# A quarter of k's transfers on GpSimd's queue, the last stores on SyncE's, and another order of the same work in an attention + feed-forward kernel

## The chip, the cores and the metric

The kernel runs on one core of a Trainium2 chip. The metric is the device time of one execution in microseconds (us), taken as the median of several runs. Lower is better.

## The reference

Attention runs inside chunks of 64 tokens, without a mask, for 8 batches of 8 heads, 576 tokens of 64 numbers each. Its output becomes a matrix x of 4608 tokens by 512, and x goes through a feed-forward layer with a sigmoid form of gelu. All arrays are float32.

```python
q_c = q.reshape(B, H, nc, chunk, D)          # B, H, S, D = 8, 8, 576, 64; chunk = 64, nc = 9
...
scores = scale * np.matmul(q_c, k_c.transpose(0, 1, 2, 4, 3))
scores = scores - np.max(scores, axis=-1, keepdims=True)
attn = np.exp(scores)
attn = attn / (np.sum(attn, axis=-1, keepdims=True) + 1e-09)
out = np.matmul(attn, v_c)
...
x = np.ascontiguousarray(attn_out.transpose(0, 2, 1, 3)).reshape(B * S, H * D)     # 4608 x 512
h = x @ w_in                                                                       # 512 x 2048
g = h * (1.0 / (1.0 + np.exp(-1.702 * h)))
return (g @ w_out).astype(np.float32)                                              # 2048 x 512
```

## The kernel before

**Tiling.** The 4608 tokens are 36 tiles of 128, and nine blocks of four tiles. A float32 product is made from three matmuls on a high and a low part of each operand (lines 1129 to 1131, 1166 to 1168 and 696 to 698). The inner dimension of 2048 is cut into 16 slices. Block n and slice j have the number g = 16 n + j. For each g there is a first product h_g (x times w_in, in the halves `h0_g` and `h_g` of six matmuls), its gelu and split (`gh_g` on ScalarE, `gl_g` on VectorE), and four second products `o_g_t` (three matmuls each, t is the tile of 128 tokens), which add up in the accumulators `po_t` over the 16 slices. At the end of a block `ob_n_t` copies an accumulator to SBUF (ScalarE for even t, VectorE for odd t) and `st_n_t` stores it. Blocks 0 to 2 work in this way. Blocks 3 to 8 are taken two at a time: seven products `P1` to `P7` replace the eight of two blocks and two slices, with weight sums that were prepared (`psum`, `phi`, `plo`), written to the DRAM tensor `seven` (`pout`, `pouts`), and read back piece by piece (`ld`). The drains of these products are called `d0` to `d6`.

**Attention.** Tiles 0 to 3 are done one by one at the start. From tile 4 on they go in pairs, u = 4, 6, ..., 34, so the fourth pair is u = 10. For a pair from u = 6 on, q and k come from DRAM in pieces of 32 by 32 numbers (`qk_0_n_u` is quarter n of q, `qk_1_n_u` quarter n of k; a quarter is four transfers, and eight for u = 16 and 26), VectorE transposes each of the two (`tq0_u` for q, `tq1_u` for k, line 893), TensorE makes the scores (`s_u`, together with the product with v of the pair before), VectorE and ScalarE the softmax (`mx`, `m`, `ex`, `z`), GpSimd divides by the sums (`n_u`, line 939), and VectorE transposes the result (`et0` to `et`, line 958). There is one buffer `raw` for q and k, one for v and one for the transposed pair. So a pair's loads can start only after `tq1` of the pair before. The two PSUM buffers `hp` hold h_g: `h0_g` can start only when `gl_(g-2)` has read its buffer.

**Order.** All steps go into a planner (`Plan`). It keeps a clock per engine with costs written in the code and takes from the ready steps the one with the lowest rank. `ORDER` writes out the first part of each engine's order, and `NUDGE` changes single ranks. What comes out is one fixed order per engine, and each engine works through its own order one by one. "DMA" in the planner is SyncE's queue (SP). SP issues every load and the traffic with `seven`; its transfers share eight semaphores in turn, and a transfer waits until the eighth before it has landed. GpSimd issues the output's stores.

```python
st["raw"] = const.tile([P, 2, NP, 8, 32], F32, tag=raw_tag, name=f"raw_{u}")
...
nc.gpsimd.dma_start(out[b * S + s : b * S + s + c, :], ob[o : o + c])
```

Of the kernel before, what the change touches and what calls it, by code (L numbers as in the profile page):

```python
# [9 lines left out]
F32 = mybir.dt.float32  # L10
# [16 lines left out]
    ),  # L27
    ACT: (
# [13 lines left out]
        "k_1 q_1 k_0 q_0 q_2 k_2 q_3 k_3 raw_0 v_1 v_0 v_2 raw_1 v_3 raw_3 raw_2 rows0_4 "  # L42
        "raw_4 raw_5 raw_7 raw_8 v0_4 v1_4 raw_6"
# [4 lines left out]
class Plan:  # L48
# [9 lines left out]
    ISSUE, LANES, LANDING = 0.48, 8, 1.8  # L58
    PIECES = 3072
    TABLE_LOAD = 1.3  # L60

    def __init__(self, buffers):
        self.free = dict(buffers)
        self.steps = []
        self.landed = [0.0] * self.LANES
        self.flight = []
        self.first = {}
        self.nudge = {}


    def add(self, engine, cost, rank, fn, need=(), make=None, take=(), give=(), table=None, port=False, after=0.0):
        rank += self.nudge.get(make, 0.0)
        self.steps.append((engine, cost, rank, fn, tuple(need), make, tuple(take), tuple(give), table, port or (engine == POOL and not after), after))
# [18 lines left out]
    def emit(self):  # L92
        waits, users, ready = {}, {}, {e: [] for e in self.HANDOVER}
        at = []
# [16 lines left out]
        while left:  # L111
            for e, heap in ready.items():
                while heap and busy[e] <= now + 1e-9:
# [13 lines left out]
                    _, cost, _, fn, _, make, take, give, tab, port, after = self.steps[pick]  # L127
# [18 lines left out]
                    if e != DMA:  # L146
                        post(done, 1, (make, e, True))
                    post(done + self.HANDOVER[e], 1, (make, e, False))
# [24 lines left out]
def tile_chunk_attention_ffn(  # L173
# [38 lines left out]
    RLATE = 0  # L212

    NUDGE = {
# [4 lines left out]
    }  # L219
    ON_POOL = ()  # L220
# [590 lines left out]
    def plan_pair(u):  # L811
        st = {}
        ev = lambda n: f"{n}_{u}"
        pe = u < NPE
        NG = 2 * NP * 2
# [10 lines left out]
        def load_qk(i, n):  # L826

            if i == n == 0:
                st["raw"] = const.tile([P, 2, NP, 8, 32], F32, tag=raw_tag, name=f"raw_{u}")
            t, src = st["raw"], (q, k)[i]  # L830
            at = list(spans(u * P, 2 * P))
            if len(at) == 4:
                b, s = at[0][:2]
                for h in range(2):
                    for d in range(2):
                        p0 = h * 64 + d * 32
                        for half in range(2):
                            c = s + 32 * half
                            nc.sync.dma_start(
# [6 lines left out]
            for b, s, o, c in at:  # L846
                for h in range(2):
                    for d in range(2):
                        p0 = h * 64 + d * 32
                        nc.sync.dma_start(  # L850
# [158 lines left out]
        rank = RANKS[(u - TB) // 2]  # L1009
        if pe:  # L1010
# [290 lines left out]
```

## Time and profile before

| What | Value |
|---|---|
| median of 3 runs (lowest, highest) | 835.79 us (835.48, 837.0) |
| the profiled execution's own time | 833.93 us |
| span of its trace, from the first to the last instruction | 832.2 us |
| TensorE busy in the span | 815.4 us (98%) |
| VectorE, ScalarE, GpSimd busy | 524.4, 370.4, 103.8 us |
| mean granted TensorE clock | 0.998 |

The 1.7 us between the span and the execution's own time lie around the program. TensorE counts as busy from a matmul's start to its modelled end, and one matmul's end overlaps the next one's start; so the distance from start to start shows the pace better than the busy time does. SPq and POOLq are the issuing queues of SyncE and GpSimd. A line with "idle before <-X" says how long the engine had stood idle and what released it. The trace names a tile and not a step, so the steps named in the text follow from the order of the program: "g_l<-hp,g_h" is a `gl`, "qkT<-raw" a `tq`.

### The profile page before, as it was taken

Reading aid. Unit: us, or ns where it says so; the run is one execution under the profiler, and the core shown is the slowest. Engines: PE = TensorE matmul, PEld = TensorE weight load, DVE = VectorE, ACT = ScalarE, POOL = GpSimd, SP = SyncE. Lnnn points to the kernel's source line nnn. Section 1 sums busy time; section 2 is a strip of 40 time slices with the busy share of each in tenths; the row PEclk is TensorE's granted clock in tenths of the full one; section 3 lists DMA queues with packets and bytes.
Section 4 is the critical chain, followed back from the end, with each engine's and each line's share of the span. In section 5 each row is a group of like instructions: output and inputs, shape, how many; then the busy total and the mean of one; then the engine's idle time right before and its main releaser. Section 6 shows DMA issues by size and latency. Waiting matters only on the chain.

```text
span 832.2 us, 14752 instructions
## 1 busy us (share of the span) xinstructions
PE 815.4 (98%) x5750; PEld 674.1 (81%) x5750; DVE 524.4 (63%) x725; ACT 370.4 (45%) x545; POOL 103.8 (12%) x114
## 2 busy tenths in 40 slices
PE   8999998999999999999999999999999999999997
PEld 7888887888887888888888887888888888888786
DVE  5878975564467869874858677867568343434322
ACT  5989824433435537423436244443354223232321
POOL 1000071000166411000001010000011010000101
PEclk9999999999999999999999999999999999999999
DMA  9997855432385456755665237664440054443101
GB/s 255 327 314 209 256 143 116 73 63 34 75 257 130 147 138 202 159 163 152 157 155 154 39 87 203 159 157 128 123 141 13 14 168 131 130 118 99 50 1 50
DMA packets 231332, 114.23 MB, mean 137 GB/s; under 512 B 185952, under 2 KB 208480, under 8 KB 231264
## 3 DMA queue, kind: packets, MB, share of 16 engines
q1 hardware_dynamic: 228320, 103.86, 47.6%
q0 software_dynamic: 2944, 9.44, 3.0%
q8 instruction: 45, 0.74, 0.4%
q14 instruction: 23, 0.19, 0.1%
HBM read 89.13 MB, written 24.12 MB: 136 GB/s over the span
## 4 chain that ended last, share of the span: by engine, by line
PE 60%; issue 20%; SPq 11%; DMA 4%; DVE 2%; ACT 2%; POOL 1%; POOLq 0%; DVEq 0%; ACTq 0%
PE po L1166 10%; PE po L1167 10%; PE po L1168 10%; PE hp L696 6%; PE hp L697 6%; PE hp L698 6%; SPq L850 4%; PE hp L1129 3%; PE hp L1131 3%; PE hp L1130 3%; SPq L274 2%; SPq L354 2%; SPq L278 2%; PE s L909 2%; PE x L983 1%
## 5 line engine op out<-in xcount | busy, mean ns | idle before, releaser
L1166 PE MATMUL po<-w,g_l 128*128 128x512 f32 x576 | 226.9, 394 | 1.4 <-DVE g_l L743 0.8
L1168 PE MATMUL po<-w,g_h 128*128 128x512 f32 x576 | 224.4, 390 | 0.0
L1167 PE MATMUL po<-w,g_h 128*128 128x512 f32 x576 | 224.3, 389 | 0.0
L1166 PEld LDWEIGHTS po<-w,g_l 128*128 128x128 f32 x576 | 108.2, 188 | 26.2 <-DVE g_l L743 2.6
L1168 PEld LDWEIGHTS po<-w,g_h 128*128 128x128 f32 x576 | 108.1, 188 | 22.9
L1167 PEld LDWEIGHTS po<-w,g_h 128*128 128x128 f32 x576 | 108.3, 188 | 21.7
L734 ACT ACTIVATE g<-g 128x512 f32<-128x512 f32 x48 | 30.2, 632 | 137.8 <-DVE g L681 137.6
L696 PE MATMUL hp<-w,w 128*128 128x512 f32 x224 | 87.2, 389 | 0.3 <-DVE f L681 0.3
L698 PE MATMUL hp<-w,w 128*128 128x512 f32 x224 | 87.1, 389 | 0.0
L697 PE MATMUL hp<-w,w 128*128 128x512 f32 x224 | 87.1, 389 | 0.0
L958 DVE STREAM_TRANSPOSE eT<-e 32x512 f32<-32x512 f32 x120 | 84.2, 701 | 3.0 <-POOL e L939 1.2
L1129 PE MATMUL hp<-x_l,w 128*128 128x512 f32 x184 | 72.6, 394 | 4.4 <-DVE g_l L1156 4.4
L1131 PE MATMUL hp<-x_h,w 128*128 128x512 f32 x184 | 72.3, 393 | 0.0
L1130 PE MATMUL hp<-x_h,w 128*128 128x512 f32 x184 | 72.1, 392 | 0.0
L1185 POOL DMA_DIRECT2D out_dram<-ob x39 | 21.7, 557 | 400.3 <-ACT ob L1178 361.6
L939 POOL TENSOR_TENSOR e<-e,r 128x1024 f32<-128x1024 f32 x16 | 31.2, 1952 | 287.5 <-DVE r L936 170.5
L743 DVE TENSOR_TENSOR g_l<-g,g_h 128x512 fp32r<-128x512 f32 x48 | 33.4, 697 | 52.8 <-ACT g_h L739 52.7
L739 ACT ACTIVATE g_h<-g 128x512 fp32r<-128x512 f32 x48 | 30.3, 632 | 76.2 <-PE po L1168 69.6
L893 DVE STREAM_TRANSPOSE qkT<-raw 128x1024 f32<-128x1024 f32 x30 | 37.2, 1241 | 33.7 <-DMA raw<-in_k_dram 18.0
L1156 DVE TENSOR_TENSOR g_l<-hp,g_h 128x512 fp32r<-128x512 f32 (+1 forms) x50 | 33.2, 666 | 38.1 <-ACT g_h L1151 37.8
L1150 ACT ACTIVATE hp<-hp 128x512 f32<-128x512 f32 (+1 forms) x50 | 28.4, 569 | 47.9 <-PE hp L1131 37.8
L696 PEld LDWEIGHTS hp<-w,w 128*128 128x128 f32 x224 | 42.0, 188 | 9.4 <-DVE f L681 0.7
(118 smaller groups left out, 1224.6 us busy)
## 6 DMA issues: line engine op xcount, KB each, us to landing
w<-seven SPq DMA_DIRECT2D x112, 256.0 KB, 2.9
pieces<-seven SPq DMA_DIRECT2D x56, 256.0 KB, 2.9
seven<-w SPq DMA_DIRECT2D x24, 512.0 KB, 3.7
raw<-in_moe_w_in_dram SPq DMA_DIRECT2D x16, 512.0 KB, 7.3
raw<-in_moe_w_out_dram SPq DMA_DIRECT2D x16, 512.0 KB, 7.3
out_dram<-ob POOLq DMA_DIRECT2D x31, 256.0 KB, 2.6
raw<-in_q_dram SPq DMA_DIRECT2D x208, 32.0 KB, 2.2
raw<-in_k_dram SPq DMA_DIRECT2D x208, 32.0 KB, 2.1
```

The source lines that it names most:

```text
L696: nc.tensor.matmul(hp, w[:, 0, c], xl[:, c], start=c == 0, stop=False)
L697: nc.tensor.matmul(hp, w[:, 0, c], xh[:, c], start=False, stop=False)
L698: nc.tensor.matmul(hp, w[:, 1, c], xh[:, c], start=False, stop=c == 1)
L743: nc.vector.tensor_tensor(gl, words(h, late), gh.bitcast(F32), op=ALU.subtract)
L893: nc.vector.transpose(st["tr"][:, i].rearrange("p n (t j) -> p (n t) j", j=32), st["raw"][:, i].rearrange("p n t j -> p (n t) j"),)
L958: nc.vector.transpose(st["et"][po : po + 32, :, 32 * a : 32 * a + 32], st["e"][pi : pi + 32, :, 32 * b : 32 * b + 32],)
L1129: nc.tensor.matmul(hp, wh, xl, start=cc == 0, stop=False)
L1130: nc.tensor.matmul(hp, wh, xh, start=False, stop=False)
L1131: nc.tensor.matmul(hp, wl, xh, start=False, stop=cc == NCC - 1)
L1166: nc.tensor.matmul(po, gl[:, c], w[:, 0, :], start=first, stop=False)
L1167: nc.tensor.matmul(po, gh[:, c], w[:, 0, :], start=False, stop=False)
L1168: nc.tensor.matmul(po, gh[:, c], w[:, 1, :], start=False, stop=last)
```

## The change

From pair u = 10 on the last quarter of k (n = 3) is issued on GpSimd's queue, in single transfers `qkp_..._u` that the planner places on GpSimd: 4 for most pairs, 8 for u = 16 and 26, 60 in all. The four stores of the last block go to SP. The planner has other costs for issue and landing, and a model of GpSimd's queue. A shift for whole pairs (`SHIFT`) and 35 more entries in `NUDGE` give another order of the same steps on all engines. No computing step is added or removed.

```diff
-    ISSUE, LANES, LANDING = 0.48, 8, 1.8
+    ISSUE, LANES, LANDING = 0.495, 8, 1.9
     PIECES = 3072
+    RING = 3
...
+                    if late:
+                        cost += max(0.0, self.ring[-self.RING] - now)
+                        late += min(3.1, max(0.0, 0.5 * (self.landed[-1] - now - cost - 2.0)))
+                        self.ring.append(now + cost + late)
...
+    POOLED, POOL_FROM = 1, 10
...
+        "wj_13": 14, "qk_0_3_10": -6, "o_127_1": -4, "pa0_4": 5, "o_86_1": -12, "P7_0_0": 8,
...
+    SHIFT = {10: 3.5, 8: 2.0, 26: -12.5, 12: 4.0, 34: -12.5, 6: 3.0}
...
+        pooled = POOLED * (u >= POOL_FROM)
...
+        def load_qk(i, n, hd, only=None):
+            queue = nc.gpsimd if i and n >= NP - pooled else nc.sync
...
-                            nc.sync.dma_start(
+                            queue.dma_start(
...
+                    for x in range(4 * count):
+                        parts[i].append(ev(f"qkp_{8 * n + x}"))
+                        plan.add(
+                            POOL, 0.59, rank - ahead - RLATE,
+                            lambda i=i, n=n, x=x: load_qk(i, n, HD[x // count : x // count + 1], x % count if count > 1 else None),
+                            need=[ev("rawt")], make=parts[i][-1], late=1.95,
+                        )
...
-        def o_store(t):
+        def o_store(t, queue):
...
-                nc.gpsimd.dma_start(out[b * S + s : b * S + s + c, :], ob[o : o + c])
+                queue.dma_start(out[b * S + s : b * S + s + c, :], ob[o : o + c])
...
+                if n == NB - 1:
+                    plan.add(DMA, (count, 0.85, 128), rank - STORE, lambda t=t: o_store(t, nc.sync), **store)
+                else:
+                    plan.add(POOL, 0.56 * count, rank - STORE, lambda t=t: o_store(t, nc.gpsimd), after=2.6, late=2.6, **store)
```

Three places of the order follow, each before and then with the change. **VectorE at pair u = 10**, in block 1: `qkT` is the transposed pair, and the two `g_l` ahead of `z` are `gl_16` and `gl_17`.

```order
L926 TENSOR_TENSOR e_1436<-s_1361,m_1437 128x1024
L893 STREAM_TRANSPOSE qkT_1496<-raw_1335 128x1024
L1156 TENSOR_TENSOR g_l_1499<-hp_1466,g_h_1498 128x512
L1156 TENSOR_TENSOR g_l_1525<-hp_1489,g_h_1524 128x512
L933 TENSOR_REDUCE z_1550<-e_1436 128x16
```

With the change, at the same place:

```order
L942 TENSOR_TENSOR e_1440<-s_1364,m_1441 128x1024
L1187 TENSOR_TENSOR g_l_1503<-hp_1472,g_h_1502 128x512
L909 STREAM_TRANSPOSE qkT_1525<-raw_1349 128x1024
L1187 TENSOR_TENSOR g_l_1528<-hp_1495,g_h_1527 128x512
L949 TENSOR_REDUCE z_1551<-e_1440 128x16
```

The first `g_l` (`gl_16`) now stands ahead of q's transpose `tq0_10`; the second (`gl_17`) still stands behind it.

**SP's queue at pair u = 18**, at the end of block 1's loads: `raw` is this pair's q and k, `pieces`, `w` and `seven` are the traffic of the weight sums.

```order
L850 DMA raw_2394<-in_k_dram 32x8x32 x8
L687 DMA pieces<-seven 128x2x256 x2
L689 DMA w_328<-seven 128x512 x2
L689 DMA w_440<-seven 128x512 x2
L617 DMA seven<-w_530 128x1024
L617 DMA seven<-w_543 128x1024
L850 DMA raw_2394<-in_k_dram 32x8x32 x4
L354 DMA v_2680<-in_v_dram 64x8x64 x2
```

With the change, at the same place:

```order
L866 DMA raw_2382<-in_k_dram 32x8x32 x4
L701 DMA pieces<-seven 128x2x256 x2
L703 DMA w_328<-seven 128x512 x2
L703 DMA w_440<-seven 128x512 x2
L631 DMA seven<-w_530 128x1024
L631 DMA seven<-w_543 128x1024
L368 DMA v_2680<-in_v_dram 64x8x64 x2
```

The last four transfers of k, which stood behind six reads from `seven` and two writes to it, are gone from SP. On GpSimd they stand ahead of block 1's first store and of `n_14`. In VectorE's order `tq1_18` has moved from behind `m_16` to ahead of `mx_16`.

**TensorE where blocks 7 and 8 meet**: `po_3` is `o_127_3`, the last second product of block 7 for tile 3. The rows behind it belong to block 8, whose slices 14 and 15 (`o_142`, `o_143`) come first.

```order
L1166 MATMUL po_3_6783<-w_1216,g_l_7471 128x512
L1167 MATMUL po_3_6783<-w_1216,g_h_7470 128x512
L1168 MATMUL po_3_6783<-w_1216,g_h_7470 128x512
L1166 MATMUL po_1_7503<-w_1132,g_l_7481 128x512
L1167 MATMUL po_1_7503<-w_1132,g_h_7480 128x512
L1168 MATMUL po_1_7503<-w_1132,g_h_7480 128x512
L1166 MATMUL po_0_7495<-w_1216,g_l_7508 128x512
```

With the change, at the same place:

```order
L1197 MATMUL po_3_6783<-w_1181,g_l_7465 128x512
L1198 MATMUL po_3_6783<-w_1181,g_h_7464 128x512
L1199 MATMUL po_3_6783<-w_1181,g_h_7464 128x512
L1197 MATMUL po_2_7499<-w_1145,g_l_7492 128x512
L1198 MATMUL po_2_7499<-w_1145,g_h_7491 128x512
L1199 MATMUL po_2_7499<-w_1145,g_h_7491 128x512
L1197 MATMUL po_1_7506<-w_1145,g_l_7492 128x512
L1198 MATMUL po_1_7506<-w_1145,g_h_7491 128x512
L1199 MATMUL po_1_7506<-w_1145,g_h_7491 128x512
L1197 MATMUL po_1_7506<-w_1181,g_l_7504 128x512
```

Between `o_127_3` and the first product with `gl_143` there was one product of `o_142` and are now two. A little ahead of this, behind `P4` of the last slice, five second products stand in front of the first one with `gl_127`, where four stood.

## Rows read from the trace of the kernel before

**Rows 1.** The waits of TensorE: us in total, times, longest.

```profile
PE hp L1129 <- DVE g_l L1156: 4.4, 2, 2.6
...
PE po L1166 <- DVE g_l L743: 0.8, 1, 0.8
...
PE hp L696 <- DVE f L681: 0.3, 1, 0.3
```

**Rows 2.** TensorE's timeline around the first gap: start, length, line, tile.

```profile
125.00 0.39 PE L1131 MATMUL hp<-x_h,w 128*128 128x512 f32 x1
...
128.40 0.39 PE L1131 MATMUL hp<-x_h,w 128*128 128x512 f32 x1
131.36 0.50 PE L1129 MATMUL hp<-x_l,w 128*128 128x512 f32 x1 [2.57 <-DVE g_l L1156]
...
136.03 0.40 PE L1167 MATMUL po<-w,g_h 128*128 128x512 f32 x1
```

**Rows 3.** Busy time by stretch behind that gap; PEclk is the granted clock.

```profile
132.00:136.00 4.00, 4.00 (x12) 3.13 (x11) 1.65 (x3) 1.84 (x3) 1.69 (x1) 0.58 0.39 64
```

**Rows 4.** VectorE's timeline in the first gap.

```profile
129.48 1.25 DVE L893 STREAM_TRANSPOSE qkT<-raw 128x1024 f32<-128x1024 f32 x1 [4.28 <-DMA raw<-in_k_dram]
130.65 1.25 DVE L1156 TENSOR_TENSOR g_l<-hp,g_h 128x512 fp32r<-128x512 f32 x2
```

**Rows 5.** SP's and GpSimd's timelines ahead of it.

```profile
116.20 10.27 SPq L850 DMA_DIRECT2D raw<-in_q_dram  x16
126.51 7.99 SPq L850 DMA_DIRECT2D raw<-in_k_dram  x16
...
116.14 2.54 POOL L581 TENSOR_TENSOR whole<-w 128x512 f32<-128x512 f32 x2
```

**Rows 6.** Line 850 from 116 to 135 us: its transfers' time to landing.

```profile
DMA to landing us min/median/max: 1.8/2.1/4.4
```

**Rows 7.** TensorE's timeline at the second gap.

```profile
250.69 0.39 PE L1168 MATMUL po<-w,g_h 128*128 128x512 f32 x1
252.87 0.50 PE L1129 MATMUL hp<-x_l,w 128*128 128x512 f32 x1 [1.79 <-DVE g_l L1156]
```

**Rows 8.** VectorE's timeline at the second gap.

```profile
249.79 1.25 DVE L893 STREAM_TRANSPOSE qkT<-raw 128x1024 f32<-128x1024 f32 x1 [4.36 <-DMA raw<-in_k_dram]
```

**Rows 9.** SP's timeline ahead of it, and line 850's landing from 240 to 252 us.

```profile
241.44 4.02 SPq L850 DMA_DIRECT2D raw<-in_k_dram  x4
...
DMA to landing us min/median/max: 1.7/4.7/7.6
```

**Rows 10.** TensorE's timeline where blocks 7 and 8 meet.

```profile
778.46 0.39 PE L1168 MATMUL po<-w,g_h 128*128 128x512 f32 x1
778.96 0.50 PE L1166 MATMUL po<-w,g_l 128*128 128x512 f32 x1
...
782.97 0.39 PE L1168 MATMUL po<-w,g_h 128*128 128x512 f32 x1
...
784.13 0.50 PE L1166 MATMUL po<-w,g_l 128*128 128x512 f32 x1 [0.77 <-DVE g_l L743]
```

**Rows 11.** The end: VectorE's last copy and GpSimd's last store.

```profile
827.03 0.69 DVE L1180 COPY ob<-po 128x512 f32<-128x512 f32 x1 [0.67 <-PE po L1168]
828.13 0.55 POOL L1185 DMA_DIRECT2D out_dram<-ob  x1 [0.16 <-issue]
```

**Rows 12.** The page's DMA issues: count, KB each, median us to landing.

```profile
out_dram<-ob POOLq DMA_DIRECT2D x31, 256.0 KB, 2.6
...
seven<-w SPq DMA_DIRECT2D x8, 256.0 KB, 3.6
```

**Rows 13.** Line 1185, all stores from GpSimd: ns min/median/max of an issue.

```profile
L1185 POOL DMA_DIRECT2D out_dram<-ob x39: 534/542/728, 122.3 to 828.1; - x39
```

**Rows 14.** VectorE's and GpSimd's timelines at pair u = 16: `tq1_16` and `n_14`.

```profile
217.86 1.25 DVE L893 STREAM_TRANSPOSE qkT<-raw 128x1024 f32<-128x1024 f32 x1 [1.87 <-DMA raw<-in_k_dram]
...
227.15 1.90 POOL L939 TENSOR_TENSOR e<-e,r 128x1024 f32<-128x1024 f32 x1 [0.54 <-DVE r L936]
```

More of the change, by code (lines that the diff above doesn't have):

```diff
@@ L66, in __init__, with add @@
         self.flight = []
+        self.ring = [0.0] * self.RING
         self.first = {}
         self.nudge = {}
-    def add(self, engine, cost, rank, fn, need=(), make=None, take=(), give=(), table=None, port=False, after=0.0):
-        rank += self.nudge.get(make, 0.0)
-        self.steps.append((engine, cost, rank, fn, tuple(need), make, tuple(take), tuple(give), table, port or (engine == POOL and not after), after))
+        self.shift = 0.0
+    def add(self, engine, cost, rank, fn, need=(), make=None, take=(), give=(), table=None, port=False, after=0.0, late=0.0):
+        rank += self.nudge.get(make, 0.0) + self.shift
+        self.steps.append((engine, cost, rank, fn, tuple(need), make, tuple(take), tuple(give), table, port or (engine == POOL and not late), after, late))
     def bulk(self, cost, rank, fn, need=(), make=None, take=(), give=()):
@@ L126, in emit @@
                         break
-                    _, cost, _, fn, _, make, take, give, tab, port, after = self.steps[pick]
+                    _, cost, _, fn, _, make, take, give, tab, port, after, late = self.steps[pick]
                     if first.get(e):
@@ L146, in emit @@
                     if e != DMA:
-                        post(done, 1, (make, e, True))
-                    post(done + self.HANDOVER[e], 1, (make, e, False))
+                        post(done + late, 1, (make, e, True))
+                    post(done + late + self.HANDOVER[e], 1, (make, e, False))
                     if e == DMA:
@@ L824, in load_qk_rows, with raw_tile @@
             load_rows(st["raw"][:, t], u + t, (q, k))
[L826 to L829 removed]
+        def raw_tile():
+            st["raw"] = const.tile([P, 2, NP, 8, 32], F32, tag=raw_tag, name=f"raw_{u}")
+        def load_qk(i, n, hd, only=None):
+            queue = nc.gpsimd if i and n >= NP - pooled else nc.sync
             t, src = st["raw"], (q, k)[i]
@@ L833, in load_qk @@
                 b, s = at[0][:2]
-                for h in range(2):
-                    for d in range(2):
+                for h, d in hd:
+                    if True:
                         p0 = h * 64 + d * 32
-                        for half in range(2):
+                        for half in range(2) if only is None else (only,):
                             c = s + 32 * half
-                            nc.sync.dma_start(
+                            queue.dma_start(
                                 t[p0 : p0 + 32, i, n, half::2, :],
@@ L845, in load_qk @@
                 return
-            for b, s, o, c in at:
-                for h in range(2):
-                    for d in range(2):
+            for b, s, o, c in at if only is None else at[only : only + 1]:
+                for h, d in hd:
+                    if True:
                         p0 = h * 64 + d * 32
-                        nc.sync.dma_start(
+                        queue.dma_start(
                             t[p0 : p0 + 32, i, n, o // 32 : (o + c) // 32, :],
@@ L1229, in plan_ffn @@
                 )
-                plan.add(
-                    POOL, 0.7 * len(list(spans((n * TB + t) * P, P))), rank - STORE, lambda t=t: o_store(t), need=[f"ob_{n}_{t}"],
-                    make=f"st_{n}_{t}", give=[tag], after=3.2,
-                )
+                count = len(list(spans((n * TB + t) * P, P)))
+                store = dict(need=[f"ob_{n}_{t}"], make=f"st_{n}_{t}", give=[tag])
+                if n == NB - 1:
+                    plan.add(DMA, (count, 0.85, 128), rank - STORE, lambda t=t: o_store(t, nc.sync), **store)
+                else:
+                    plan.add(POOL, 0.56 * count, rank - STORE, lambda t=t: o_store(t, nc.gpsimd), after=2.6, late=2.6, **store)
     def keep_warm(pool, tag, count):
```

32 lines of the change are left out of this document (21 added, 11 removed), and 24 rows, old and new, of tables (NUDGE, ORDER).

## The prediction

> **What bounds the kernel now.** I read the page first: TensorE is busy for 98% of the span, so time can come only from places where it stands or runs slowly, and I looked for those in its list of waits, then in its timeline from start to start. Between waits it is packed: fifteen intervals between 125.00 and 128.40 us give 3.40 / 15 = 0.227 us for each 128x512 matmul [rows 2]. That pace is the floor of all computing, and the change removes no matmul. Behind 40 us the timeline leaves it at four places only; some 6 us more are lost in the start, whose order the change hardly touches, and I put those at nothing either way.
>
> **Place A, block 1, pair u = 10.** TensorE starts a matmul at 128.40 and the next, the first of `h0_18`, at 131.36; it waited 2.57 us for a `gl` [rows 2]. From 128.40 to 136.03 it does 14 intervals, which take 14 x 0.227 = 3.17 us at the pace: 7.63 - 3.17 = 4.46 us are lost. The pause itself is 2.96 - 0.23 = 2.73 of that. The rest is the clock: after the pause the granted clock is 0.58 of full in 132 to 136 us, the lower of two levels (1.2 instead of 2.4 GHz) for most of it [rows 3]. VectorE shows what is late: the transpose `tq0_10` starts at 129.48 after 4.28 us of idle, released by a transfer, and `gl_16` and `gl_17` start behind it at 130.65 (1.25 us for the two) [rows 4]. The row names k's tile line, but both transposes have that line; it is the first one, so it waits for q. SP issued q's sixteen transfers from 116.20 for 10.27 us, then k's for 7.99 us [rows 5], and a transfer lands a median of 2.1 us behind its issue [rows 6]. So a `gl` whose own inputs were there stood in VectorE's queue behind a transpose that waited for a DMA.
>
> **Place B, block 2, pair u = 18.** The pause from 250.69 to 252.87 is 2.18 us, 2.18 - 0.23 = 1.95 lost [rows 7]. Here `tq1_18` starts at 249.79 after 4.36 us of idle, waiting for k [rows 8], and `gl_36` is behind it. SP issued k's last four transfers from 241.44 for 4.02 us, and in this stretch the median landing is 4.7 us and the longest 7.6 [rows 9], against 2.1 at A: they stand behind reads and writes of `seven`.
>
> **Places C and D.** A drain of a seven-product group holds TensorE 0.3 us once [rows 1]. Where blocks 7 and 8 meet, the starts 778.46 to 778.96 and 782.97 to 784.13 are 0.50 and 1.16 us apart, so 0.27 and 0.93 are lost; both are waits for a `gl` [rows 10]. A, B, C and D together: 4.46 + 1.95 + 0.3 + 1.20 = 7.9 us; I take this as what order can win.
>
> **The change part by part.** *VectorE at A.* `gl_16` is now ahead of `tq0_10`, so it runs when its own operand is there, and `h0_18` can start at its slot, 128.40 + 0.23 = 128.63. The next to be held is `h0_19`, by `gl_17`, which still stands behind `tq0_10`. Between the starts of `h0_18` and `h0_19` are 24 matmuls, 5.44 us, so it wants `gl_17` by 134.07. In SP's new order the last transfer of q is the 21st behind 116.20 (a quarter of k and one load of v stand in between). At 0.50 to 0.64 us each (7.99 / 16 and 10.27 / 16) [rows 5] it is issued by 126.7 to 129.6 and lands 2.1 later, at 128.8 to 131.7 [rows 6]; with 1.25 for `tq0_10` and 0.63 for a `gl` [rows 4], `gl_17` is done at 130.7 to 133.6. That is 0.5 to 3.4 us early. Only with the longest landing of 4.4 us at the slow pace would it be late, by 1.8 us. I take the whole 4.46; the lower bound is 4.46 - 1.8 - 1.7 (the clock's part again) = 1.0.
>
> *The queues.* Each pair from u = 10 on takes four issues from SP (eight twice), some 4 x 0.50 = 2.0 us of its queue [rows 5]; thirteen pairs, 60 transfers. At B they were just those behind `seven`. On GpSimd they may start when `tq1_16` has ended, 217.86 + 1.25 = 219.11 [rows 14], 22 us before SP issued them, and `tq1_18` now stands ahead of `mx_16`. I take the whole 1.95. The lower bound is nothing, if another quarter of k, still on SP, lands as late.
>
> *The price on GpSimd.* No row shows this engine issuing a transfer of 256 short pieces. Nearest are its 39 stores of rows, 534 to 728 ns for an issue [rows 13]. The lower bound is the median, 0.54 us; the upper, for twice as many pieces, 2 x 0.54 = 1.1. I take 0.7, nearer to the same engine's rows than to the double. Four of them are 2.8 us (bounds 2.2 and 4.4). What hides it: at A GpSimd is done with its sum at 116.14 + 2.54 = 118.68 [rows 5], and the quarter is needed only when SP's 30 other transfers have landed, at 116.20 + 30 x 0.50 + 2.1 = 133.3 at the earliest; 14 us are free for 2.8. In the steady part what is queued behind these transfers is the division `n` of the pair before, ahead of `et` on VectorE and so of a pair's tiles. For u = 18 `tq1_16` ends at 219.11 and `n_14` starts at 227.15, released by VectorE [rows 14]: 8.0 us, so up to 2.0 us an issue cost nothing. I put GpSimd's share at 0.
>
> The Trainium skill, page "SBUF — State Buffer", sections "SBUF: two separate sides" and "Who interferes with whom", speaks against this edit: a DMA that GpSimd issues can be starved by some VectorE copies, with a figure of about 3.1 us instead of 0.62. The trace agrees only with the smaller figure, since none of 39 issues took over 0.728 us [rows 13]. By the page's larger figure the sum would lose the estimate of the first rival below.
>
> *D.* Five second products instead of four now stand ahead of the first with `gl_127`: each is 3 x 0.227 = 0.68 us, more than the 0.27 lost. Ahead of `gl_143`'s first reader stand two instead of one, and of the 0.93 remain 0.93 - 0.68 = 0.25. Sum 0.27 + 0.68 = 0.95; the new first product wants its own `gl_142`, which may wait 0.2. I take 0.9, bounds 0.5 and 1.2. C I leave as it is: 0, bounds 0 and 0.3.
>
> *The end.* The last copy ends at 827.03 + 0.69 = 827.72 and its store starts on GpSimd at 828.13, 0.41 later [rows 11]. SP starts the next store at up to 0.4 us sooner; a transfer of 256 KB lands 2.6 us behind GpSimd's issue, and 3.6 behind SP's of another kind, to `seven` [rows 12]. Bounds -0.4 and +1.0 - 0.4 = +0.6. SP's write is also slow where others share the queue, and at the end nothing does; I take a gain of 0.1.
>
> *The sum.* 4.46 + 1.95 + 0.9 + 0 + 0.1 = 7.4 us. The new order moves hundreds of steps, and a fixed order meets waits that it did not foresee: before, the three small ones (0.3, 0.27, 0.93) [rows 1, 10] are of 0.3 to 0.9. I allow one mean one, (0.3 + 0.27 + 0.93) / 3 = 0.5, and forecast -6.9 us. Against the profiled execution of 833.93 us that is 827.0; the median of the runs is 835.79, 1.86 above it, and I give the forecast against the median: 835.79 - 6.9 = 828.9.
>
> **The rivals.** *GpSimd's issue is slow (slower than before).* Place: every pair's `n` behind up to four transfers. The point from which it decides is the 2.0 us an issue worked out above. At 3.1, say, four take 12.4, so `n` comes 4.4 us late, `et` waits on VectorE with every `gl` behind it, and TensorE loses about 3 us, the size of A's pause (2.73). Nine `n` stand so in the new order; four hit are 12 us, and 835.8 - 7.4 + 12 = 840.4. Against it: 728 ns is the longest issue seen [rows 13]. For it: these transfers have other shapes, and no row shows them. A chance of 0.12.
>
> *The wait only moves (partial).* TensorE comes to everything behind A some 4.5 us earlier, behind B 6.4, while loads come at SP's pace: then `gl_17`, or a later `gl` behind a transpose, waits. If A gives 1.0 of 4.46 the sum is 7.4 - 3.5 = 3.9 and with the allowance 3.4, so 832.4; the case spans 830.5 to 834. For it: 0.5 us of margin at A by the slow pace. Against it: SP has 2 us less to issue for each pair. A chance of 0.25.
>
> *Nothing comes of it.* If all loads bind as soon as TensorE is ahead, what A and B give is lost again at the next pairs: 835.8. Against it: only at A do the loads fill SP's time; from `tq1_16`'s end at 219.11 to the last issue for u = 18 at 241.44 + 4.02 lie 26 us [rows 9, 14], and 32 issues of 0.50 would fill 16. A chance of 0.06.
>
> *The likeliest*: A, B and most of D are removed and the new waits are small: 828.9, its own range 826.0 (all 7.9 us, against the profiled execution's 833.93) to 830.5 (1.6 us of waits more than I allow). A chance of 0.57.
>
> **The numbers.** Below 830.5 lies 0.57, and 0.25 up to 834.1. A range from 825.5 (0.4 more at the end) to 834.0 leaves out about 0.02 below and 0.18 above. About 0.2% (1.7 us) is what a measurement of this kernel can tell from no change. Faster by that means below 834.1: 0.57 + 0.24 = 0.81. Same: 0.06 and the ends of the partial and slow cases, 0.08. Slower: 0.11.
>
> **What would show it.** In the profile after: the row of `hp` waiting for `gl` gone or under 0.5 us; the granted clock full from 40 us to the end; `tq0_10` and `tq1_18` with `gl_16` and `gl_36` no longer behind their idle time; the transfers of `raw` on GpSimd's queue at 0.54 to 1.1 us an issue; starts where blocks 7 and 8 meet 0.23 to 0.5 apart. The prediction is wrong if GpSimd's issues take over 2 us or `n` waits behind them; if a stretch behind 128 us still shows the clock near 0.6; or if a new row of 1 us or more stands among TensorE's waits.

## The result, and the profile after

| What | before | with the change |
|---|---|---|
| median (lowest, highest), 4 runs each | 835.75 us (835.48, 837.0) | 824.55 us (824.06, 828.46) |
| ratio, 95% interval | | 0.9873 (0.9842 to 0.9905) |
| the profiled execution's own time | 833.93 us | 828.46 us |
| span of its trace | 832.2 us | 826.7 us |

The change makes the kernel 11.2 us faster, 1.3%; 6.9 us were forecast, and 824.55 lies below the range. In two ways the profiled executions are not the typical ones: that of the kernel before is 1.8 us faster than its median, that of the changed kernel 3.9 us slower. So a second trace of the changed kernel (the run after_again below, 824.53 us) is read beside the first.

TensorE's waits in the changed kernel's first trace, the rows behind the start (engine, line, releaser: us in total, times, longest):

```profile
PE hp L1160 <- DVE g_l L1187: 1.5, 2, 0.9
...
PE qkTp L891 <- DMA rows<-in_q_dram: 1.1, 1, 1.1
...
PE po L1197 <- DVE g_l L1187: 0.2, 1, 0.2
```

and in after_again:

```profile
PE po L1197 <- DVE g_l L1187: 0.5, 1, 0.5
PE hp L1160 <- DVE g_l L1187: 0.3, 1, 0.3
```

The 4.4 us of `hp` waiting for `gl` [rows 1] are 1.5 and 0.3 now. Two of the prediction's signs fail in the first trace (1.5 us where under 0.5 was expected, and a new row of 1.1 us, in the start); in after_again both hold. The page's row of the granted clock is full in all 40 slices of both kernels, since a slice is 20 us long, so a stretch has to be read. In the changed kernel's first trace the clock (the third number from the end) is 1.00 from 124 to 150 us, where [rows 3] have 0.58 for four of these:

```profile
124.00:150.00 26.00, 25.41 (x111) 20.55 (x111) 16.11 (x23) 11.38 (x17) 6.49 (x9) 1.00 0.54 116
```

**A.** VectorE's timeline at pair u = 10 of the changed kernel's first trace, then TensorE's start of `h0_19`:

```profile
130.80 0.69 DVE L1187 TENSOR_TENSOR g_l<-hp,g_h 128x512 fp32r<-128x512 f32 x1 [2.14 <-ACT g_h L1182]
135.58 1.25 DVE L909 STREAM_TRANSPOSE qkT<-raw 128x1024 f32<-128x1024 f32 x1 [4.09 <-DMA raw<-in_q_dram]
136.75 0.65 DVE L1187 TENSOR_TENSOR g_l<-hp,g_h 128x512 fp32r<-128x512 f32 x1
...
137.29 0.39 PE L1199 MATMUL po<-w,g_h 128*128 128x512 f32 x1
137.52 0.45 PE L1160 MATMUL hp<-x_l,w 128*128 128x512 f32 x1
```

Q's transpose still waits 4.09 us for its transfer, as long as before [rows 4]. But `gl_16` has run ahead of it, and `gl_17` behind it ends at 137.40, in time for `h0_19` at 137.52, which starts 0.23 us behind the matmul ahead of it.

**B.** VectorE at pair u = 18, changed kernel, first trace:

```profile
241.77 2.37 DVE L909 STREAM_TRANSPOSE qkT<-raw 128x1024 f32<-128x1024 f32 x2 [2.46 <-PE s L925]
...
247.01 0.69 DVE L565 TENSOR_TENSOR w<-xs,w 128x512 fp32r<-128x512 f32 x1 [0.50 <-DMA seven<-w]
247.62 0.68 DVE L565 TENSOR_TENSOR w<-g,w 128x512 fp32r<-128x512 f32 x1
248.23 0.69 DVE L1187 TENSOR_TENSOR g_l<-hp,g_h 128x512 fp32r<-128x512 f32 x1
```

`tq0_18` and `tq1_18` run in one go and no transfer holds them (before: 4.36 us [rows 8]). A new releaser stands one row down: a write to `seven` holds the next step for 0.50 us. It comes back below.

**GpSimd's queue.** The groups of its transfers, of 32 KB each in line 866 and of 16 KB (u = 16 and 26) in line 855 (busy us, mean ns of one, idle before and what ended it), and the timeline at u = 18:

```profile
L866 POOL DMA_DIRECT2D raw<-in_k_dram x44 | 26.3, 600 | 151.7 <-DMA v<-in_v_dram 80.3 <-DVE qkT L909 40.0 <-DMA w<-seven 22.6
...
L1216 POOL DMA_DIRECT2D out_dram<-ob x35 | 19.4, 557 | 294.7 <-DVE ob L1211 222.8 <-ACT ob L1209 70.0 <-issue 1.0
L855 POOL DMA_DIRECT2D raw<-in_k_dram x16 | 8.8, 557 | 36.9 <-DMA v<-in_v_dram 19.4 <-DVE qkT L909 17.4
```

```profile
244.55 1.80 POOL L866 DMA_DIRECT2D raw<-in_k_dram  x3 [0.42 <-DVE qkT L909]
248.36 0.58 POOL L866 DMA_DIRECT2D raw<-in_k_dram  x1 [2.00 <-issue]
```

An issue of 32 KB takes 0.60 us in the mean, hardly more than a store's 0.56 or the 0.56 of 16 KB. At u = 18 three go at once; the fourth starts 2.00 us after the third is done.

**D and the end.** TensorE where blocks 7 and 8 meet, the last copy on ScalarE and the last stores on SP:

```profile
778.66 0.39 PE L1199 MATMUL po<-w,g_h 128*128 128x512 f32 x1
779.14 0.50 PE L1197 MATMUL po<-w,g_l 128*128 128x512 f32 x1
...
823.02 0.60 ACT L1209 ACTIVATE ob<-po 128x512 f32<-128x512 f32 x1 [1.44 <-PE po L1199]
...
821.02 2.95 SPq L1216 DMA_DIRECT2D out_dram<-ob  x4
```

Of three pauses one is left, 0.48 - 0.23 = 0.25 us. The last copy ends at 823.62 and the span at 826.7: 3.1 us, where they were 832.2 - 827.72 = 4.5 [rows 11].

**Place by place.** From the traces I summed, for each stretch, what TensorE's starts lie apart beyond the pace of their shape (scores and transposes have some of this in both kernels, so only differences count). Three traces of the kernel before (833.93, 834.27 and 833.59 us) stand beside after_again (824.53 us):

| stretch, us | before, three traces | after_again | gained against the mean |
|---|---|---|---|
| 124 to 200 (A) | 7.39, 8.09, 8.26 | 3.49 | 4.4 |
| 200 to 260 (B) | 4.96, 4.92, 4.43 | 2.88 | 1.9 |
| 480 to 520 (C) | 2.30, 1.98, 1.90 | 1.47 | 0.6 |
| 760 to 800 (D) | 2.02, 2.05, 1.99 | 0.54 | 1.5 |
| 260 to 480 | 8.75, 8.75, 8.86 | 9.26 | -0.5 |
| last matmul's start to the end | 5.56, 5.56, 5.53 | 4.06 | 1.5 |

The sum is 9.4, and so is the difference of the spans (832.2, 832.5 and 831.8, mean 832.2, to 822.7: 9.5); the stretches left out differ by 0.3 us at most (the first 124 us lose 18.5 to 18.8 in all four traces). The changed kernel's first trace is 3.9 us longer than this one, and 3.6 of that lie in the first 124 us, where it loses 22.2 us against 18.6, with waits at 53 and 96 us.

### The profile page after: what moved, and what is told of

Its sections match the earlier page's. It is cut to its first block, busy times and chain, and to the rows that moved or that the text cites. A ratio compares the mean times of both kernels' runs of the same rounds, so it can differ in the third digit from the quotient of the medians.

```text
span 826.7 us, 14873 instructions
## 1 busy us (share of the span) xinstructions
PE 814.1 (98%) x5750; PEld 673.2 (81%) x5750; DVE 525.8 (64%) x725; ACT 370.9 (45%) x545; POOL 137.7 (17%) x170
## 4 chain that ended last, share of the span: by engine, by line
PE 82%; SPq 9%; DMA 4%; ACT 2%; DVE 2%; issue 1%; POOL 0%; DVEq 0%
PE po L1197 14%; PE po L1199 14%; PE po L1198 14%; PE hp L710 9%; PE hp L712 9%; PE hp L711 9%; PE hp L1160 3%; PE hp L1161 3%; PE hp L1162 3%; DMA raw<-in_moe_w_out_dram 3%; SPq L368 2%; SPq L288 2%; SPq L866 2%; PE s L925 2%; PE x L999 2%; SPq L292 1%
## 5 line engine op out<-in xcount | busy, mean ns | idle before, releaser
L1216 POOL DMA_DIRECT2D out_dram<-ob x35 | 19.4, 557 | 294.7 <-DVE ob L1211 222.8
L866 POOL DMA_DIRECT2D raw<-in_k_dram x44 | 26.3, 600 | 151.7 <-DMA v<-in_v_dram 80.3
L710 PEld LDWEIGHTS hp<-w,w 128*128 128x128 f32 x224 | 42.0, 188 | 8.9 <-ACT d L723 0.2
L712 PEld LDWEIGHTS hp<-w,w 128*128 128x128 f32 x224 | 42.0, 188 | 8.7
```

What stands on the lines that cost most here:

```text
L710: nc.tensor.matmul(hp, w[:, 0, c], xl[:, c], start=c == 0, stop=False)
L712: nc.tensor.matmul(hp, w[:, 1, c], xh[:, c], start=False, stop=c == 1)
L866: queue.dma_start(t[p0 : p0 + 32, i, n, o // 32 : (o + c) // 32, :], src[b, 2 * n + h, s : s + c, d * 32 : d * 32 + 32].rearrange("(t j) i ...
```

## The experiments

Where steps are moved, a pass behind the planner takes its finished order of each engine and moves the named steps; all others keep their places. Times of the kernel before differ between the chips and from execution to execution (medians of 832.7 to 835.79 us, single executions from 827.9 to 838.5), so kernels are compared by their ratio to the executions of before beside them (a median of 832.7 us for the first four of the table, 835.2 for the next six, 835.0 for the last two; each of these three groups ran on a chip of its own). A difference of two medians across groups is given with that of the ratios.

| kernel | median us | ratio to before, 95% interval |
|---|---|---|
| before_gl16 | 830.35 | 0.9976 (0.9953 to 1.0) |
| a_old_order | 831.42 | 0.9972 (0.9953 to 0.9991) |
| k_on_sp | 828.81 | 0.9936 (0.9912 to 0.9959) |
| st_pool | 826.60 | 0.9909 (0.9878 to 0.994) |
| after_again | 824.89 | 0.9879 (0.985 to 0.9908) |
| before_pool | 836.74 | 1.0026 (1.0002 to 1.005) |
| after_plus | 824.55 | 0.9876 (0.9845 to 0.9908) |
| before_b | 834.31 | 0.9998 (0.9968 to 1.0028) |
| before_abd | 829.59 | 0.9938 (0.9915 to 0.996) |
| k_two_quarters | 825.36 | 0.9889 (0.9845 to 0.9932) |
| pool_early | 832.72 | 0.998 (0.9959 to 1.0002) |
| abd_pool | 825.25 | 0.9892 (0.9866 to 0.9918) |

### Is A a matter of VectorE's order?

before_gl16, the kernel before:

```diff
+    MOVE = [('gl_16', 'before', 'tq0_10')]
```

> The kernel before, with one step moved: the VectorE step gl_16 stands ahead of the transpose tq0_10 instead of behind it. Theory (the pause at A is a matter of VectorE's order alone): h0_18 no longer waits, gl_17 is ready before h0_19 wants it, the clock stays full in 128 to 140 us, and the kernel gains the 4.5 us lost at A: 835.75 - 4.5 = 831.3 us. Rival (q comes too late anyway): the wait moves to h0_19, the clock still falls, and the gain is under 1.5 us: above 834.2 us.

a_old_order, the changed kernel:

```diff
+    MOVE = [('gl_16', 'after', 'tq0_10')]
```

> The changed kernel, with gl_16 put back behind tq0_10 and all else as changed. Theory (order alone decides A): the pause comes back, and as q of u = 10 now lands later than in the kernel before, it is at least as long: 4.5 to 6.5 us with the clock's part, 829 to 831 us. Rival (the change wins at A for another reason, earlier transfers say): under 1 us is lost, below 825.6 us.

The stretch 132 to 136 us in before_gl16, where [rows 3] show 0.58 (the granted clock is the third number from the end):

```profile
132.00:136.00 4.00, 4.00 (x20) 3.30 (x19) 3.10 (x5) 2.28 (x3) 1.90 (x1) 1.00 0.72 156
```

VectorE at A in before_gl16, then in before_abd (a kernel further below that has the same move and others):

```profile
126.74 0.69 DVE L1187 TENSOR_TENSOR g_l<-hp,g_h 128x512 fp32r<-128x512 f32 x1 [2.14 <-ACT g_h L1182]
127.35 1.23 DVE L924 STREAM_TRANSPOSE qkT<-raw 128x1024 f32<-128x1024 f32 x1
```

```profile
127.52 0.69 DVE L1187 TENSOR_TENSOR g_l<-hp,g_h 128x512 fp32r<-128x512 f32 x1 [2.14 <-ACT g_h L1182]
130.29 1.25 DVE L924 STREAM_TRANSPOSE qkT<-raw 128x1024 f32<-128x1024 f32 x1 [2.08 <-DMA raw<-in_k_dram]
```

VectorE at A in a_old_order, and its clock:

```profile
132.28 1.25 DVE L940 STREAM_TRANSPOSE qkT<-raw 128x1024 f32<-128x1024 f32 x1 [7.03 <-DMA raw<-in_q_dram]
133.45 1.25 DVE L1218 TENSOR_TENSOR g_l<-hp,g_h 128x512 fp32r<-128x512 f32 x2
```

```profile
132.00:136.00 4.00, 1.84 (x4) 1.49 (x5) 3.69 (x5) 1.73 (x2) 0.00 (x0) 0.66 0.52 91
136.00:140.00 4.00, 4.00 (x11) 3.10 (x10) 2.93 (x5) 0.32 (x1) 3.28 (x4) 0.50 0.12 21
```

When q is late, one step of 0.65 us decides whether TensorE stops. Put back in the changed kernel it brings a pause of 5.5 us and costs 831.42 - 824.89 = 6.5 us (7.8 by the ratios), more than the 4.5 at A before, because q lands later in the new order (132.28 against 129.48) and the clock is down for longer. The trace of before_gl16 alone shows less than its full clock suggests: in this execution, the fastest of its twelve (828.33 us), `tq0_10` starts at 127.35 without waiting, so q was there 2 us and more sooner than in the three traces of the kernel before (129.48, 130.12 and 130.05), and the old order would have held `gl_16` for little. The move is seen at work in before_abd: `tq0_10` waits for q until 130.29, `gl_16` has run ahead of it at 127.52, and TensorE has no pause before 139 us. In the kernel before the move gains 2.4 us of the median (0 to 3.9) where 4.5 were expected and the rival said under 1.5, so the time decides for neither; the mechanism rests on a_old_order and before_abd.

### Is GpSimd's queue needed?

k_on_sp is the changed kernel with all of k on SP; before_pool the kernel before with the same quarter on GpSimd, at its old place in the work.

```diff
-            queue = nc.gpsimd if i and n >= NP - pooled else nc.sync
+            queue = nc.sync
```

> The changed kernel with its order on every engine, but all 60 transfers of k that went to GpSimd are issued by SP, at their places in the order of work. Theory (the second queue matters): SP falls behind by 2 us for each pair where loads are close to the bound, gl_17 behind tq0_10 becomes late at A by about 1.5 us, and so does a pair in blocks 1 and 2: 2 to 4 us slower than the changed kernel, 826.5 to 828.5 us. Rival (the order alone did it, the queue is hidden): within 0.5 us of 824.55.

```diff
+            queue = nc.gpsimd if i and n == NP - 1 and u >= 10 else nc.sync
...
-                            nc.sync.dma_start(
+                            queue.dma_start(
```

> The kernel before, its order kept on every engine, with the last quarter of k from u = 10 on issued by GpSimd at its old place in the work (4 transfers a pair, 8 twice). Theory (the queue helps only where k waits behind other traffic): B's 1.95 us are gone or under 0.5, A stays, since it waits for q: 1 to 2 us faster than the kernel before. Rival (the queue is what wins at A as well): 4 us or more faster. Second rival (issues on GpSimd are slow, over 2 us each): slower than the kernel before.

VectorE at A in k_on_sp, then GpSimd and VectorE at B in before_pool:

```profile
134.58 1.25 DVE L909 STREAM_TRANSPOSE qkT<-raw 128x1024 f32<-128x1024 f32 x1 [5.99 <-DMA raw<-in_q_dram]
135.75 0.65 DVE L1187 TENSOR_TENSOR g_l<-hp,g_h 128x512 fp32r<-128x512 f32 x1
```

```profile
242.01 1.86 POOL L851 DMA_DIRECT2D raw<-in_k_dram  x3 [0.40 <-DMA w<-seven]
248.37 0.58 POOL L851 DMA_DIRECT2D raw<-in_k_dram  x1 [4.51 <-issue]
...
250.61 1.25 DVE L894 STREAM_TRANSPOSE qkT<-raw 128x1024 f32<-128x1024 f32 x1 [5.14 <-DMA raw<-in_k_dram]
```

Without the queue the new order loses 4 us (828.81 against 824.89; 4.8 by the ratios): `gl_17` is late as expected, a pause of 1.9 us at 134.4, and smaller ones follow at 142, 161 and 250 us. This is an order made for two queues with one taken away; an order planned for SP alone was not tried. With the queue but at the old places nothing is gained; the median is 0.3% higher. GpSimd reaches the four transfers as late as SP did, three go, and the fourth stands 4.51 us: the longest such pause in any trace, in a stretch where the four took a median of 5.5 us to land. So a second queue alone does not help, it must also be used early.

### Is B a matter of order?

before_b, the kernel before:

```diff
+    MOVE = [('qk_1_3_18', 'before', 'ld0_0_0'), ('tq1_18', 'before', 'mx_16')]
```

> The kernel before, all of it on SP, with two steps moved at B only: the last quarter of k of u = 18 ahead of the reads of seven on SP, and tq1_18 ahead of mx_16 on VectorE. Theory (B is a matter of the order on SP and VectorE, no second queue is needed): the pause at 251 us is under 0.5 us, and the kernel is 1.5 to 2 us faster than the kernel before. Rival (without GpSimd's queue something else stands in front, the reads of seven that are now later say): a pause of 1 us or more between 245 and 275 us, and no gain.

VectorE in before_b, and the landing of what SP issued from 240 to 252 us:

```profile
242.80 2.37 DVE L924 STREAM_TRANSPOSE qkT<-raw 128x1024 f32<-128x1024 f32 x2 [2.46 <-PE s L940]
...
251.93 0.69 DVE L582 TENSOR_TENSOR w<-xs,w 128x512 fp32r<-128x512 f32 x1 [4.38 <-DMA seven<-w]
252.53 0.68 DVE L582 TENSOR_TENSOR w<-g,w 128x512 fp32r<-128x512 f32 x1
253.14 0.68 DVE L1187 TENSOR_TENSOR g_l<-hp,g_h 128x512 fp32r<-128x512 f32 x1
```

```profile
seven<-w SPq DMA_DIRECT2D x2, 512.0 KB, 7.2
```

The theory falls. K no longer holds anything, and the pause is as long as before: `l0x_0_0`, directly behind, waits 4.38 us for a write to `seven` to land, which SP issued behind k and which takes a median of 7.2 us. Two waits lay on top of each other at B, k's and `seven`'s, and an order on one queue can only choose which of them comes last.

pool_early, the kernel before with the quarter on GpSimd and at early places:

```diff
+    MOVE = [('qk_1_3_10', 'before', 'st_0_0'), ('qk_1_3_12', 'after', 'n_8'), ('qk_1_3_14', 'after', 'qk_1_3_12'),
+            ('qk_1_3_16', 'before', 'n_12'), ('qk_1_3_18', 'before', 'st_1_0'), ('qk_1_3_20', 'before', 'n_16'),
...
+            queue = nc.gpsimd if i and n == NP - 1 and u >= 10 else nc.sync
```

> The kernel before with its order, except that the last quarter of k from u = 10 on is on GpSimd as early as the changed kernel has it: as soon as the pair before has left the buffer, ahead of that block's stores and divisions. Theory (the second queue gives SP time: 2 us a pair, and the writes to seven behind it start and land earlier): the pause at B goes to under 0.5 us, A stays at 4 to 5 us, since q of u = 10 is issued as before; 2 to 3 us faster than the kernel before, a ratio of 0.9965 to 0.9975. Rival (without the new order the queue gives nothing, as with the transfers at their old places): a ratio of 0.999 or more and a pause at B of 1.5 us or more.

As expected, no pause of over 0.15 us is left from 200 to 260 us, and that at A is as before. The time says less: the median is 2.3 us lower, but the ratio of 0.998 lies between the theory's 0.9975 and the rival's 0.999, and its interval reaches past 1. TensorE's waits in pool_early:

```profile
PE hp L1160 <- DVE g_l L1187: 3.0, 1, 3.0
```

### Do the places add up?

before_abd is the kernel before, all loads on SP, with the moves at A and B, the order of the changed kernel where blocks 7 and 8 meet, and the end; abd_pool has the queue of pool_early as well (and at B only `tq1_18` moved).

```diff
+    MOVE = [('gl_16', 'before', 'tq0_10'), ('qk_1_3_18', 'before', 'ld0_0_0'), ('tq1_18', 'before', 'mx_16'),
+            ('P3_2_7', 'before', 'o_125_2'), ('P4_2_7', 'before', 'o_125_2'), ('gl_126', 'after', 'd5_2_7'),
...
+            ('o_140_0', 'after', 'o_141_3'), ('o_141_0', 'after', 'o_140_0'), ('ob_8_0', 'after', 'ob_8_2'),
...
-                nc.gpsimd.dma_start(out[b * S + s : b * S + s + c, :], ob[o : o + c])
+                (nc.sync if n == NB - 1 else nc.gpsimd).dma_start(out[b * S + s : b * S + s + c, :], ob[o : o + c])
```

> The kernel before, no transfer of k on GpSimd, with single steps moved at four places only: gl_16 at A; the two moves of before_b at B; where blocks 7 and 8 meet the order of second products, copies and drains of the changed kernel; at the end the last copies in the changed kernel's order and the four last stores on SP. Theory (the gain is the sum of these places, A 4.6, B 2.0, D 1.5, end 1.5 by the differences of the traces): 9.6 us faster than the kernel before, a ratio of 0.9885, within 1 us of the changed kernel. Rival (GpSimd's queue is needed as well, as the kernel with all of k on SP was 4 us slower): 5 to 7 us faster, a ratio of 0.992 to 0.994, with new waits of 2 us or more between 124 and 260 us.

> The kernel before with the moves of before_abd (A, tq1_18 at B, blocks 7 and 8, the end with its stores on SP) and the last quarter of k early on GpSimd as in pool_early. Theory (at A the order removes the first wait and the queue the one behind it, so that both together give what the change gives): the waits at 139, 160 and 250 us of before_abd are under 0.7 us each, and the ratio is 0.986 to 0.989, within 1.5 us of the changed kernel. Rival (the rest of the new order, the shifts of whole pairs, is needed too): a ratio of 0.991 or more, with over 2.5 us of waits left between 124 and 260 us.

VectorE in before_abd behind A:

```profile
137.98 1.25 DVE L924 STREAM_TRANSPOSE qkT<-raw 128x1024 f32<-128x1024 f32 x1 [3.65 <-DMA raw<-in_k_dram]
139.15 1.37 DVE L989 STREAM_TRANSPOSE eT<-e 32x512 f32<-32x512 f32 x2
140.55 0.69 DVE L1187 TENSOR_TENSOR g_l<-hp,g_h 128x512 fp32r<-128x512 f32 x1
...
159.51 1.25 DVE L924 STREAM_TRANSPOSE qkT<-raw 128x1024 f32<-128x1024 f32 x1 [3.35 <-DMA raw<-in_k_dram]
160.68 0.65 DVE L1187 TENSOR_TENSOR g_l<-hp,g_h 128x512 fp32r<-128x512 f32 x1
```

and TensorE's waits for `gl` in before_abd, then in abd_pool:

```profile
PE hp L1160 <- DVE g_l L1187: 3.5, 3, 1.5
PE po L1197 <- DVE g_l L1187: 0.5, 1, 0.5
```

```profile
PE po L1197 <- DVE g_l L1187: 0.4, 1, 0.4
```

before_abd gains 5.6 us of the 9.6: the rival holds. Freed at A, TensorE meets the next transposes that wait, now of k: pauses of 1.6, 1.4 and 1.0 us at 139, 160 and 250 us, 4.0 in all. With the queue these are gone, and abd_pool is at 825.25, within 0.4 us of after_again and with an interval that holds its ratio. So 22 moved steps, the last stores on SP and the early queue are nearly all of the change; the shifts of whole pairs and the rest of the new order show no gain here that this measurement can tell.

### The end, the second trace, the double and one more attempt

```diff
-                    plan.add(DMA, (count, 0.85, 128), rank - STORE, lambda t=t: o_store(t, nc.sync), **store)
+                    plan.add(DMA, (count, 0.85, 128), rank - STORE, lambda t=t: o_store(t, nc.gpsimd), **store)
```

> The changed kernel with the last block's four stores on GpSimd's queue again, all else as changed. The prediction's term for the end was 0.1 us. Theory from the two traces (the execution ends 4.45 us behind the last copy's end before and 3.04 behind it after): 1.2 to 1.5 us slower, 825.8 to 826.1 us. Rival (the end is bound by the landing of 256 KB on either queue): within 0.3 us of 824.55.

ScalarE's last copy in st_pool:

```profile
820.01 0.60 ACT L1209 ACTIVATE ob<-po 128x512 f32<-128x512 f32 x1 [1.44 <-PE po L1199]
```

It ends at 820.61 and the span at 824.5: 3.9 us, against 3.1 with SP and 4.5 before. So 0.8 us of the end's gain is the queue, and 0.6 comes with the new order of the last copies (no run has that order alone). The median is 1.7 us above after_again's (2.5 by the ratios), but its interval reaches 2.6 us to either side and the trace has another wait of 1.4 us at 93 us, so its time alone settles nothing.

after_again and before_again are the two kernels as they are; before_third was another trace of the kernel before.

> The changed kernel as it is, to see how its time and its waits differ from execution to execution, beside the kernel before. Theory (what differs is only when the first loads land: the waits at 53, 83, 96 and 143 us of its first trace, 3.7 us in all, are absent from a typical execution): a median of 824 to 825.5 us, and a trace with under 2 us of waits behind 40 us. Rival (the four runs of the result were a lucky draw): a median of 826 us or more with these waits in the trace.

> The kernel before as it is, for a second trace of it. Theory (the pause at A depends on when q lands, the others stand in the order): A differs from the first trace's 4.5 us by a microsecond or more, while the pauses at 501, 778, 783 and 788 us are the same to 0.1 us. Rival (every pause differs alike, or what differs is the start): A within 0.5 us of 4.5, the start up to 40 us off by more than A.

> The kernel before as it is, for a third trace. Theory (its executions differ by A and B, whose pauses depend on landings and pull the clock down when they are long): the time follows the loss between 124 and 260 us, to within 1 us, when set against the two traces there are (833.93 and 834.27 us). Rival (they differ at the start or somewhere else): the time differs by over 1 us with the same loss there.

The changed kernel's median is 824.89, and its trace has 0.8 us of waits for `gl`: the theory. In the kernel before, the starts across A lie 2.74, 3.40 and 3.60 us beyond the pace in the three traces, across B 1.95, 1.92 and 1.41, and D's three agree to 0.01 us; C differs too (one pause of 0.45 us in the first, none above 0.15 in the others), which the expectation had among the fixed ones. A differs by 0.9 us, just under the microsecond expected. The three executions lie within 0.7 us of each other, so they can't show what makes others 829 or 838.

```diff
-            queue = nc.gpsimd if i and n >= NP - pooled else nc.sync
+            queue = nc.gpsimd if i and n >= NP - 2 * pooled else nc.sync
```

> The changed kernel with two quarters of k on GpSimd instead of one: 8 transfers a pair and 16 twice, at their places in the order of work. The first rival of the prediction put the point from which GpSimd's issues cost time at 8 us for a pair's transfers. Theory (0.59 us an issue, and each fourth waits until an earlier one has landed, so 8 take 7 to 10 us): n comes late in some pairs, 1 to 3 us slower than the changed kernel, a ratio to the kernel before of 0.989 to 0.992. Rival (SP's relief outweighs it): the same or faster than the changed kernel, 0.986 to 0.988. Second rival (the starved queue): 8 us or more slower.

k_two_quarters is 0.5 us above after_again, within the uncertainty, and its trace shows 25 pauses ahead of such issues, 27.3 us in all. Neither the theory's 1 to 3 us nor a gain can be told; the starved queue is excluded.

after_plus, the changed kernel:

```diff
+    MOVE = [('gh_10', 'before', 'wlow_14'), ('gl_10', 'before', 'wj_14'), ('gl_18', 'before', 'et0_8')]
```

> The changed kernel with three steps moved: gh_10 on ScalarE ahead of wlow_14, gl_10 on VectorE ahead of wj_14, and gl_18 ahead of et0_8. In the changed kernel's trace h0_12 (at 97 us) and h0_20 (at 143.8 us) wait 1.1 and 0.75 us for these. Theory (these are waits of order alone, and nothing else is due there): both waits are gone and the kernel is 1.0 to 1.9 us faster than the changed one. Rival (the transfers bind next, so the wait moves to a later step): under 0.5 us, with another wait of about the same size within two pairs.

In time the rival holds: 0.3 us lower, which can't be told from nothing. The waits it removes are not in a typical execution (after_again has 0.43 us at 139 us, none at 93), and its own trace has one of 0.6 us at 133 us. No version here beats the change.

## Why the prediction was wrong

The mechanism held, as far as the runs test it: late transfers held ready work on VectorE, and order and queue removed that. The step that failed is the sizing of the sum outside A and B: the end was put at 0.1 us and measured 1.5, D at 0.9 and measured 1.5, C at nothing and measured 0.6; and the sum was taken from a median that lies 1.9 us above the execution it was worked out for.

- **A, 4.46 us: right in size, incomplete in mechanism.** The traces give 4.4. That `gl_16` ahead of `tq0_10` is what keeps TensorE going is shown both ways where q is late (before_abd, a_old_order). That `gl_17` comes "0.5 to 3.4 us early" was too kind: it had 0.1 us in the first trace and 0.3 in after_again (done at 133.64, wanted at 133.94), so that it came in time was close. And with the order alone the wait moves to the next pairs (before_abd, and k_on_sp at 134 us). This was the partial rival; what kept it away is SP's relief, which the prediction named against this rival without giving it a size.
- **B, 1.95 us: right in size (1.9), half right in cause.** K was one of two late transfers. before_b shows the second, the write to `seven`; pool_early shows that the relief brings both earlier.
- **GpSimd's price, 0: right.** 0.60 us an issue, where 0.7 was taken between 0.54 and 1.1. The first rival fell; its place was not empty, though, as most fourth issues of 32 KB pause, and 4.51 us of it stand in before_pool's pause at B.
- **D, 0.9 us: too small.** The traces give 1.5. The prediction counted two of three pauses and the new wait; the third (0.25 us), the drop in pace behind each pause, and `P4` of the last slice two products earlier were left out.
- **C, 0: too small.** 0.6 us, and no run shows why: only one of the three traces of the kernel before has a pause there.
- **The end, 0.1 us: the term furthest off.** It is 1.5. SP's landing was bounded by its writes to `seven`; the traces show a 256 KB store landing a median of 2.0 us behind SP's issue and 2.4 behind GpSimd's at the end. What the new order of the last copies wins, 0.6 us, was not counted at all.
- **New waits, 0.5 us: right (0.5), in part by luck.** The 0.5 is what 260 to 480 us lose; only 0.31 us of it stand as a pause in after_again, at 323 us.
- **The base: the largest single error, 1.9 us.** The sum was made against the profiled execution, 833.93, and then subtracted from the median, 835.79. Against the traces the measured terms give 833.9 - 9.4 = 824.5. That agrees with after_again's own execution by construction, but also with the median that was measured. So what the kernel before took beyond its traces in these runs is gone with the change as well. It is no fixed amount: on another chip the kernel before had a median of 832.7 us, below its three traces.

Together 828.9 - 824.55 = 4.4 us: 1.9 of the base, 1.4 of the end, 0.6 of D and 0.6 of C make 4.5. The range failed with them, since its lower end allowed only for the pauses that were counted.

**What stays open** is in part why executions of the kernel before spread over 10 us and those of the changed one over 4.7 (823.79 to 828.46 in the result's four and after_again's six). The mean granted clock of every execution is on record. Of the 82 executions of the kernel before that ran beside the experiments, the eleven with a clock of 0.999 or 1.0 took 827.9 to 832.2 us and the seventeen with 0.994 or less 834.3 to 838.5; all ten of the changed kernel have 0.999 or 1.0. So much of the spread goes with the clock, though not all: those eleven still lie 4.3 us apart. Where the clock fell in executions without a trace is not shown. In the three traces of the kernel before it fell behind A alone until the last matmul. In before_b and before_pool, profiled at 835.79 and 836.43 us, it also fell behind B; the same stretch in before_b and then in the kernel before:

```profile
256.00:260.00 4.00, 4.00 (x14) 3.11 (x14) 3.15 (x7) 3.29 (x5) 2.16 (x1) 0.71 0.56 164
```

```profile
256.00:260.00 4.00, 4.00 (x19) 3.33 (x18) 3.96 (x6) 1.62 (x3) 3.23 (x5) 1.00 0.49 96
```

That a pause at A or B which is sometimes long enough to bring the clock down, and so is paid for twice, makes the slower executions is argued from this. That q was early in the trace of before_gl16, at 828.33 us, fits it.

The Trainium skill, page "DMA: Bandwidth & Descriptors", section "Issuing engines are not separate DMA queues", says that a second issuing engine only saves the time of the issue, which it calls usually small. Here the issue is what counts: 0.45 to 0.5 us by the traces, 32 in a row for a pair, and taking four of them away from each pair was worth 4 us of the kernel by the medians (k_on_sp).

## What to carry to other kernels

An in-order engine's operation that waits for a transfer holds every ready operation behind it: move the ready one ahead, but look at what waits next, because a stall removed only brings the next late transfer to the front. A second issuing queue pays where it is given its transfers early and the first queue is bound by its number of issues; the moved steps with the last stores on SP were worth 5.6 us alone, the early queue 2.3 (with an interval that reaches nothing), and both together 9.7. Forecast from one execution's spans, but ask whether what the change removes is also what makes the other executions differ.

## What the runs showed of the hardware

- In most pairs GpSimd issued three transfers of 32 KB back to back and held the fourth, 0.7 to 2.0 us in the changed kernel's first trace and 4.51 us where the transfers took a median of 5.5 us to land (before_pool). That it waits for an earlier one to land fits these numbers and wasn't tried by itself. Eight transfers of 16 KB went without a hold (before_pool, below), so it isn't a matter of their number alone.

```profile
190.70 4.37 POOL L840 DMA_DIRECT2D raw<-in_k_dram  x8
```

- A store of 128x512 and a load of 32x8x32 cost GpSimd nearly the same issue: 557 and 600 ns in the mean (the changed kernel's first trace).
- Pauses of TensorE of 1.98 us (before_b, at B) to 5.5 us (a_old_order) were followed by 3 to 6 us of matmuls at the lower of the clock's two levels; those of 1.41 to 1.95 us at B in the three traces of the kernel before and of 1.85 us in k_on_sp were not. The two groups nearly touch, so the length of a pause alone is not shown to decide.
